# Attention and maxout in one kernel: the first half's masks as products on VectorE instead of sums on TensorE, in a new order of work

## The chip, the core and the metric

The kernel runs on one core of a Trainium2 chip. The metric is device time in microseconds; the time of a version is the median of several executions. One further execution was taken by the hardware profiler, and all rows of the profile are from that one. The engines are TensorE (PE, with its weight loads shown as PEld), VectorE (DVE), ScalarE (ACT), GpSimd (POOL) and SyncE (SP). In this kernel SP issues the transfers. They work on SBUF, and TensorE writes its results into eight PSUM banks. Each engine runs its own instructions in their written order and waits for the others at semaphores.

## What is computed

Four sequences of 768 tokens, 8 heads of 64 dimensions. Three heads are "retrieval" heads with a plain causal mask. The five others attend to a window of 64 tokens and to the first four tokens (the sinks). A maxout layer follows.

```python
scores = scale * np.matmul(q, k.transpose(0, 1, 3, 2))
causal = rel >= 0
stream_keep = causal & ((pos[None, :] < n_sink) | (rel < window))
mask = np.where(retr, causal, stream_keep)
scores = np.where(mask, scores, -1e9)
a = softmax(scores)                     # over the keys
x = (a @ v).transpose(0, 2, 1, 3).reshape(B * S, H * D)
g = np.maximum(x @ w1, x @ w2)
out = g @ w_out
```

## The kernel before

**Maxout.** max(x w1, x w2) is relu(x (w1 - w2)) + x w2. The kernel therefore prepares three weights: `w12` = w1 - w2 (four VectorE subtractions, L1184), `w2o` = w2 w_out, and `wob`, w_out in bf16. For `w2o` it casts w2 to bf16 (`w2b`), transposes it on TensorE (L1201), copies it to `w2t`, and multiplies it with `wob` (L1228, 32 matmuls in 16 steps: four banks times four quarters of `wob`). `wob` comes in quarters 0 to 3; each has its own transfer (`load_down`, L568) and its own cast, made by whichever engine the order names. A copy or cast that ScalarE does is recorded at L382, one by another engine at L384.

**Halves.** The work is done in eight halves of 384 queries, sequence by sequence or nearly: (0,0), (1,0), (0,1), (1,1), (2,0) and so on. For each half, q and k are cast to bf16, transposed (on TensorE at L680 in the first halves, by DMA later) and copied out of PSUM. Then come

- scores (`scores`, L959): key blocks by query blocks of 128, written into two banks at a time, in a number of groups t,
- exponentials (`exp`, L978, ScalarE) into the tile `at`, one per bank; no maximum is subtracted,
- masks (`mask`, L997, VectorE): `at` times a 0/1 table, in place,
- weighted sums (`weighted`, L1022, TensorE): `at` times v with a column of ones,
- the reciprocal (L1039) and the product with it (`normalise`, L1049, VectorE), which give `x`,
- the transposes of x (L1148, or by DMA), the up-projection with `w12` (`up`, L1251, eight blocks of four matmuls), the ReLU (L1276 on ScalarE or L1278 on VectorE), and the down-projection (`down`, L1308, 12 matmuls for each of three tiles of 128 rows), copied out and stored (L1336).

In the very first half the rows of v arrive in another layout; ScalarE, VectorE and GpSimd cast them into the tile `xt` (`cast_rows`, L720), and TensorE rearranges them (L723).

**Masks of the first half.** The first half (0,0) has groups of its own (`GROUP_A`). Streaming heads have blocks "near" (the diagonal and the window) and "far" (only sinks). Here no mask is multiplied: GpSimd writes tables of 0 and -1e30 into `tab` (`mask_table`, L1649 to L1662, over zeros that VectorE's memset at L1699 wrote), and TensorE puts them into the bank first, as a matmul of the identity and the table (L928). The scores then accumulate on it, and the exponential gives 0 where the table has -1e30. The other halves multiply, with 0/1 tables that GpSimd derives from the first ones by four comparisons (`kept`, L612).

**The order of work.** The order is one string, `PLAN`, written out by hand or by a search. A token such as `76p01` means operation 76 on TensorE with PSUM banks 0 and 1; a, v, g and s stand for ScalarE, VectorE, GpSimd and SP. `x0*40` means 40 dummy matmuls (L372) into bank 0: products of a zero tile, which nobody reads. `Order.run` emits the tokens one by one, so the string fixes the queue of every engine. The tables of costs and ranks beside it had a part in the search, not in what is emitted. SP's queue begins with q, k and v of the first half, and the weights follow: w2 in halves, w_out in quarters, w1 in halves. A transfer waits for the casts that free its place in the tile `ld`: w_out's quarters take the place of the first half's q, k and v.

Of the kernel before, what the change touches and what calls it, by code (L numbers as in the profile page):

```python
# [38 lines left out]
def one(p, hh, blocks):  # L39
# [16 lines left out]
B_FAR, B_NEAR, B_WIN, B_CAUSAL = 0, 2, 5, 7  # L56
GROUP_A = [
    (both(0, DIAG0 + f(0, 1)), [], [(0, 0, 1, B_CAUSAL, 3), (1, 0, 1, B_CAUSAL, 3)]),
    (
        [one(1, 0, DIAG0 + f(0, 1)), one(1, 1, NEAR)], [],  # L60
        [(0, 0, 1, B_CAUSAL, 3), (1, 0, 4, B_NEAR, 1)],
    ),
    (
        [one(0, 0, f(0, 2) + f(1, 2)) + one(1, 0, f(0, 2) + f(1, 2)),
         one(0, 1, f(0, 2) + f(1, 2)) + one(1, 1, FAR)], [], [(1, 2, 2, B_FAR, 1)],
    ),
    (both(2, NEAR), [], [(0, 0, 4, B_NEAR, 1), (1, 0, 4, B_NEAR, 1)]),
    (both(3, NEAR), [], [(0, 0, 4, B_NEAR, 1), (1, 0, 4, B_NEAR, 1)]),
    (
        [one(2, 0, FAR) + one(3, 0, FAR), one(2, 1, FAR) + one(3, 1, FAR)], [],  # L70
        [(0, 0, 2, B_FAR, 2), (1, 0, 2, B_FAR, 2)],
# [3 lines left out]
    (both(0, DIAG0 + f(0, 1)), [(0, 2, 0, 3, "causal")], []),  # L75
    (both(0, f(0, 2) + f(1, 2)), [], []),
    ([one(1, 0, DIAG0 + f(0, 1)), one(1, 1, WIN0)], [(0, 1, 0, 3, "causal"), (1, 1, 0, 4, 0)], []),
    ([one(1, 0, f(0, 2) + f(1, 2)), one(1, 1, d(2) + d(2))], [(1, 1, 0, 1, "band")], []),
    (both(2, WIN0), [(0, 2, 0, 4, 0)], []),
    (both(3, WIN0), [(0, 2, 0, 4, 0)], []),  # L80
    (
        [one(2, 0, d(2)) + one(3, 0, d(2)), one(2, 1, d(2)) + one(3, 1, d(2))],
        [(0, 2, 0, 2, "band")], [],
    ),
]
TWICE = [(0, 0, 2, B_WIN, 2), (1, 0, 2, B_WIN, 2)]
GROUP1 = [
    (
        both(0, DIAG1 + f(4, 5)), [(0, 2, 0, 3, "causal")],
        [(0, 0, 1, B_CAUSAL, 3), (1, 0, 1, B_CAUSAL, 3)],  # L90
    ),
    (both(0, f(0, 3, 4, 5) + f(3, 4)), [], []),
    (both(0, f(1, 3, 4, 5) + f(3, 5)), [], []),
    (both(0, f(2, 3, 4, 5)), [], []),
    (
        [one(1, 0, DIAG1 + f(4, 5)), one(1, 1, WIN1)], [(0, 1, 0, 3, "causal"), (1, 1, 0, 4, 2)],
        [(0, 0, 1, B_CAUSAL, 3), (1, 0, 2, B_WIN, 2)],
    ),
    ([one(1, 0, f(0, 3, 4, 5) + f(3, 4)), one(1, 0, f(1, 3, 4, 5) + f(3, 5))], [], []),
    (  # L100
        [one(1, 0, f(2, 3, 4, 5)), one(1, 1, END1 + d(5))], [(1, 1, 0, 2, 2)],
        [(1, 0, 2, B_WIN, 1)],
    ),
    (both(2, WIN1), [(0, 2, 0, 4, 2)], TWICE),
    (both(3, WIN1), [(0, 2, 0, 4, 2)], TWICE),
    (
        [one(2, 0, END1) + one(3, 0, END1), one(2, 1, END1) + one(3, 1, END1)],
        [(0, 2, 0, 4, 2)], TWICE,
    ),
# [63 lines left out]
0s x0*3 1s x0*5 2s x0*40 3s 30a 32v 68g x0*3 70a 54v x0 48p0 62a 27g x1 72p1 49v x2*4 29g 60a 73v x2 64p2 x3*2  # L173
65a x3*2 52g x3*5 8s 31a 55v x3 61g x3*2 56p3 33a 53v x4*3 4s 63a x4*2 69g x4 50p4 71a 57v x5 66p5 51a 58p6
28g x7 74p7 67a 59v x0*2 26g 76p01 75a 25g 79p23 9s 34a 37v 78a 36v 6s 35v 39a 82p45 77a 41g 85p67 84a 40a
88p10 83a 86a 13s 119v 91p54 38a 123v 89a 11s 46p6 87a 93a 42p1 47v 92a 44p7 80a 43v 16s 124p4 81a 127v 120p6
45a 131v 128p5 125a 104p2 121v 106p 94p1 90a 96p 107v 5v 95p3 10g 100p 132p7 109v 105p4 97v 101v 110p 108v
# [48 lines left out]
"""  # L226

LAST = """
1079v 1082p 1080s 1074a 1083p 1075s 1086p5 1084v 1087p 1088p 1085s 1089a 1090a
"""  # L230


# [1539 lines left out]
```

## Time and profile before

| | us |
|---|---|
| median of 3 runs | 177.53 (176.96 to 178.75) |
| the profiled execution | 178.13 |
| its span, first to last instruction | 175.6 |
| TensorE busy | 167.5, 95% |
| ScalarE busy | 123.8, 71% |
| VectorE busy | 117.6, 67% |
| GpSimd busy | 35.4, 20% |

Times in rows count from the start of the span. "Idle before" is the time that the engine stood still just before an instruction, with what ended it. A row with xN stands for N instructions: in the timeline, the first number is its start, the second the time from its first start to its last end. Matmuls overlap one another, so the time of one in a group is its own latency; what a further one costs is the growth of the group's time. The clock granted to TensorE was 1.00 in nearly every slice.

### The profile page before, as it was taken

Reading aid. Unit: us, or ns where it says so; the run is one execution under the profiler, and the core shown is the slowest. Engines: PE = TensorE matmul, PEld = TensorE weight load, DVE = VectorE, ACT = ScalarE, POOL = GpSimd, SP = SyncE. Lnnn points to the kernel's source line nnn. Section 1 sums busy time; section 2 is a strip of 40 time slices with the busy share of each in tenths; the row PEclk is TensorE's granted clock in tenths of the full one; section 3 lists DMA queues with packets and bytes.
Section 4 is the critical chain, followed back from the end, with each engine's and each line's share of the span. In section 5 each row is a group of like instructions: output and inputs, shape, how many; then the busy total and the mean of one; then the engine's idle time right before and its main releaser. Section 6 shows DMA issues by size and latency. Waiting matters only on the chain.

```text
span 175.6 us, 4870 instructions
## 1 busy us (share of the span) xinstructions
PE 167.5 (95%) x1755; PEld 102.1 (58%) x1775; DVE 117.6 (67%) x327; ACT 123.8 (71%) x278; POOL 35.4 (20%) x80
## 2 busy tenths in 40 slices
PE   7899898999999999999999999999999999999993
PEld 7755644654675575667556546664665457545542
DVE  5546997876999587778978525895895377820511
ACT  3499416899899997999589789965749479214310
POOL 6850213411304803043301004200021000000000
PEclk9999999999999999999999999999999999999999
DMA  5999999999899999997299699245997236053104
GB/s 127 333 373 385 387 381 330 196 317 301 192 197 333 253 257 212 238 227 177 65 188 232 162 258 219 59 123 134 241 248 183 50 88 243 2 151 119 65 6 179
DMA packets 77661, 36.14 MB, mean 206 GB/s; under 512 B 59202, under 2 KB 72514, under 8 KB 77634
## 3 DMA queue, kind: packets, MB, share of 16 engines
q1 hardware_dynamic: 77488, 35.73, 76.7%
q8 instruction: 15, 0.25, 0.7%
q14 instruction: 12, 0.10, 0.2%
q10 hardware_dynamic: 146, 0.07, 0.1%
HBM read 25.17 MB, written 6.29 MB: 179 GB/s over the span
## 4 chain that ended last, share of the span: by engine, by line
PE 68%; DMA 11%; ACT 6%; issue 5%; POOL 4%; SPq 3%; DVE 2%; DVEq 0%; ACTq 0%; POOLq 0%
PE ps L1308 30%; PE ps L1251 21%; PE ps L959 7%; PE ps L1022 7%; DMA ld<-in_moe_w_out_dram 6%; DMA ld<-in_v_dram 4%; ACT at L978 4%; PE ps L680 2%; SPq L455 2%; POOL wob L384 2%; PE ps L1228 1%; POOL tab L612 1%; ACT ot L382 1%; ACT vb L382 1%; DMA raw<-in_is_retrieval_dram 1%
## 5 line engine op out<-in xcount | busy, mean ns | idle before, releaser
L978 ACT ACTIVATE at<-ps 128x512 bf16<-128x512 f32 (+2 forms) x134 | 64.8, 578 | 4.6 <-PE ps L959 4.1
L1251 PE MATMUL ps<-xt,w 128*128 128x384 bf16 x256 | 45.2, 326 | 0.1
L1308 PE MATMUL ps<-wob,g 128*128 128x512 bf16 (+2 forms) x192 | 43.8, 371 | 0.7 <-issue 0.3
L997 DVE TENSOR_TENSOR at<-at,tab 128x1024 bf16<-128x1024 bf16 (+5 forms) x49 | 25.1, 524 | 12.3 <-ACT at L978 11.4
L1251 PEld LDWEIGHTS <-w 128*128 128x128 bf16 x256 | 24.0, 98 | 15.9 <-issue 0.6
L1308 PEld LDWEIGHTS <-g 128*128 128x128 bf16 x200 | 18.3, 98 | 19.6 <-issue 0.2
L1278 DVE TENSOR_SCALAR g<-ps 128x384 bf16<-128x384 f32 x34 | 18.5, 553 | 13.5 <-PE ps L1251 13.0
L382 ACT COPY ot<-ps 128x512 f32<-128x512 f32 (+1 forms) x16 | 9.0, 571 | 22.5 <-PE ps L1308 19.1
L1308 PE MATMUL ps<-w2o,xt 128*128 128x512 bf16 (+2 forms) x90 | 24.0, 370 | 0.5
L384 POOL CAST qb<-ld 128x384 bf16 (+1 forms) x31 | 13.6, 472 | 53.3 <-DMA ld<-in_k_dram 28.4
L1049 DVE TENSOR_TENSOR x<-ps,rez 128x192 f32 x64 | 22.7, 354 | 2.0 <-DVE rez L1039 0.5
L1022 PEld LDWEIGHTS <-at 128*128 128x128 bf16 x477 | 17.9, 97 | 4.7 <-DVE at L997 0.3
L1022 PE MATMUL ps<-vb,at 128*128 128x65 bf16 x387 | 19.3, 194 | 0.0
L1276 ACT ACTIVATE g<-ps 128x384 bf16<-128x384 f32 x30 | 14.5, 495 | 6.6 <-PE ps L1251 6.4
L959 PE MATMUL ps<-qk 64*128 64x128 bf16 (+1 forms) x330 | 19.1, 229 | 0.0
L959 PEld LDWEIGHTS <-qk 64*128 64x128 bf16 x330 | 12.1, 94 | 9.2 <-issue 7.0
L382 ACT CAST qb<-ld 128x384 bf16 (+1 forms) x32 | 12.8, 458 | 2.1 <-DMA ld<-in_q_dram 1.7
L1308 PEld LDWEIGHTS <-xt 128*128 128x128 bf16 x100 | 8.8, 98 | 8.1
L382 ACT COPY qk<-ps 128x384 bf16<-128x384 bf16 (+1 forms) x17 | 10.2, 631 | 2.3 <-PE ps L680 1.9
L384 DVE COPY ot<-ps 128x512 f32<-128x512 f32 (+1 forms) x9 | 6.0, 672 | 7.3 <-PE ps L1308 6.4
L680 PE MATMUL ps<-tab,qb 128*128 128x128 bf16 x120 | 10.0, 219 | 0.7 <-POOL qb L384 0.4
L384 POOL CAST vb<-ld 128x192 bf16 x15 | 6.1, 421 | 20.3 <-issue 10.2
(76 smaller groups left out, 162.7 us busy)
## 6 DMA issues: line engine op xcount, KB each, us to landing
ld<-in_v_dram SPq DMA_DIRECT2D x21, 256.0 KB, 5.4
ld<-in_moe_w_dram SPq DMA_DIRECT2D x4, 1024.0 KB, 12.2
out_dram<-ot SPq DMA_DIRECT2D x16, 256.0 KB, 3.6
ld<-in_q_dram SPq DMA_DIRECT2D x5, 768.0 KB, 8.1
ld<-in_k_dram SPq DMA_DIRECT2D x5, 768.0 KB, 6.9
ld<-in_q_dram SPq DMA_DIRECT2D x9, 256.0 KB, 4.5
ld<-in_k_dram SPq DMA_DIRECT2D x9, 256.0 KB, 4.4
ld<-in_moe_w_out_dram SPq DMA_DIRECT2D x4, 512.0 KB, 11.0
```

The source lines that it names most:

```text
L382: nc.scalar.copy(out=out, in_=in_)
L384: eng[e].tensor_copy(out=out, in_=in_)
L680: nc.tensor.transpose(to[:, i], qbs[:, T["qb", n, hf] % NQB, t, i].rearrange("p h d -> p (h d)"), ident)
L959: nc.tensor.matmul(to.rearrange("p (i c) -> p i c", c=128), lhsT=lhsT, rhs=q_of(n, i, m)[rows], start=bk not in under, stop=True, skip_gro ...
L978: nc.scalar.activation(out=at[:, bk, 0:w], in_=bank(("ps", b, hf, t), part=bk)[:, 0:w], func=ACT.Exp, scale=scale,)
L997: eng[e].tensor_tensor(out=at, in0=at, in1=tbl, op=ALU.mult)
L1022: nc.tensor.matmul(po[:, hh, i - NT * hf, :], lhsT=ats[:, T["at", b, hf, t] % NAT, bk, e * 128:(e + 1) * 128], rhs=rhs, start=first, stop= ...
L1049: nc.vector.tensor_tensor(out=xs[:, HALVES.index((b, hf)) % NX, :, bass.ds(heads[2 * p + hh], 1), :], in0=po[:, hh, :, 0:D].unsqueeze(2), ...
L1251: nc.tensor.matmul(bank(key)[:, 0:HALF], lhsT=w[:, kc, fc * 128:(fc + 1) * 128], rhs=xts[:, HALVES.index((b, hf)) % NXT, :, kc, :], start= ...
L1276: nc.scalar.activation(out=g, in_=ph, func=ACT.Relu)
L1278: nc.vector.tensor_scalar_max(out=g, in0=ph, scalar1=0.0)
L1308: nc.tensor.matmul(bank(key)[:, cols], lhsT=lhsT, rhs=(w2o if kind == "x" else wob)[:, c, cols], start=(e == 0), stop=(e == len(steps) - 1),)
```

## The change

1. The first half's masks are no longer added. The matmuls at L928 go, with the tables of -1e30, the lists of biases in the groups and `biases`. The groups of the first half name masks instead, and VectorE multiplies `at` by 0/1 tables behind the exponentials: seven new products, five of them of the new kinds "near" and "far".
2. GpSimd writes 0/1 tables at once, over ones in place of zeros, so `kept` goes. The last two copies of `mask_table` now write three blocks each. The memset of 576 words becomes one of 64 words (the identity's zeros) and one of 1280 bf16 ones.
3. `PLAN` is new from beginning to end. There are 133 dummies instead of 81. The other matmuls are the same ones, with the same sizes.

```diff
 GROUP_A = [
-    (both(0, DIAG0 + f(0, 1)), [], [(0, 0, 1, B_CAUSAL, 3), (1, 0, 1, B_CAUSAL, 3)]),
-    (
-        [one(1, 0, DIAG0 + f(0, 1)), one(1, 1, NEAR)], [],
-        [(0, 0, 1, B_CAUSAL, 3), (1, 0, 4, B_NEAR, 1)],
-    ),
+    (both(0, DIAG0 + f(0, 1)), [(0, 2, 0, 3, "causal")]),
+    ([one(1, 0, DIAG0 + f(0, 1)), one(1, 1, NEAR)], [(0, 1, 0, 3, "causal"), (1, 1, 0, 4, "near")]),
     (
         [one(0, 0, f(0, 2) + f(1, 2)) + one(1, 0, f(0, 2) + f(1, 2)),
-         one(0, 1, f(0, 2) + f(1, 2)) + one(1, 1, FAR)], [], [(1, 2, 2, B_FAR, 1)],
+         one(0, 1, f(0, 2) + f(1, 2)) + one(1, 1, FAR)], [(1, 1, 2, 2, "far")],
     ),
-    (both(2, NEAR), [], [(0, 0, 4, B_NEAR, 1), (1, 0, 4, B_NEAR, 1)]),
-    (both(3, NEAR), [], [(0, 0, 4, B_NEAR, 1), (1, 0, 4, B_NEAR, 1)]),
+    (both(2, NEAR), [(0, 2, 0, 4, "near")]),
+    (both(3, NEAR), [(0, 2, 0, 4, "near")]),
     (
-        [one(2, 0, FAR) + one(3, 0, FAR), one(2, 1, FAR) + one(3, 1, FAR)], [],
-        [(0, 0, 2, B_FAR, 2), (1, 0, 2, B_FAR, 2)],
+        [one(2, 0, FAR) + one(3, 0, FAR), one(2, 1, FAR) + one(3, 1, FAR)], [(0, 2, 0, 4, "far")],
     ),
 ]
...
 PLAN = """
-0s x0*3 1s x0*5 2s x0*40 3s 30a 32v 68g x0*3 70a 54v x0 48p0 62a 27g x1 72p1 49v x2*4 29g 60a 73v x2 64p2 x3*2
+0s x0*3 1s x0*5 2s x0*36 3s 66a 50v x0*3 28a 64v x0 48g x0 58a x0 68p0 26a 25g x1*2 52p1 56a 69v 44p2 x3 4s
...
-BIASED = ((0, 0),)
...
-    ident, bias, smask = tab[:, 0:128], tab[:, 128:1152], tab[:, 1152:1920]
-    causal = tab[:, 1920:2048]
+    ident, smask, causal = tab[:, 0:128], tab[:, 640:1408], tab[:, 512:640]
+    far, near = tab[:, 128:384], tab[:, 384:1408].rearrange("p (n two c) -> p n two c", two=2, c=128)[:, :, 0]
...
-    kept(pairs_[:, 0:1], 3)
-    kept(pairs_[:, 1:6:2], 6, times=3)
-    kept(pairs_[:, 2:6:2], 4, blocks=2)
-    kept(causal.unsqueeze(1), 7)
...
     def scores(b, hf, t):
-            for bk, e, m, col, times in biased:
-                src = bias[:, 128 * col:128 * col + 128 * m]
-                to = bank(("ps", b, hf, t), part=bk)[:, e * 128:(e + m * times) * 128]
...
-                nc.tensor.matmul(to, lhsT=ident, rhs=src, start=True, stop=False, skip_group_check=True)
...
-                        start=bk not in under, stop=True, skip_group_check=True,
+                        start=True, stop=True, skip_group_check=True,
...
     def mask(b, hf, t, part):
-            if isinstance(which, str):
+            if which == "near":
+                at = at.rearrange("p h (m c) -> p h m c", c=128)
+                tbl = near[:, 0:blocks].unsqueeze(1).to_broadcast([128, count, blocks, 128])
+            elif which == "far":
+                at = at.rearrange("p h (m c) -> p h m c", c=256)
+                tbl = far.unsqueeze(1).unsqueeze(1).to_broadcast([128, count, blocks // 2, 256])
+            elif isinstance(which, str):
...
+def mask_table(nc, table, n_sink, window):
+    blocks = table.rearrange("p (n c) -> p n c", c=128)
+    def put(which, base, by_key, by_query, fill=0.0):
+        to = blocks[:, which]
+        nc.gpsimd.affine_select(
+            out=to, in_=to, pattern=[[0, to.shape[1]], [by_query, 128]], compare_op=ALU.is_ge, fill=fill, base=base,
+            channel_multiplier=by_key,
+        )
+    sinks, both_, causal, diagonal = slice(0, 1), slice(1, 3), slice(3, 4), slice(4, 10, 2)
...
+    mixed = blocks[:, 5:10:2]
+    for rows, which in ((slice(0, 64), 0), (slice(64, 128), 1)):
+        nc.gpsimd.tensor_copy(out=mixed[rows], in_=blocks[rows, which:which + 1].to_broadcast([64, 3, 128]))
...
-    nc.vector.memset(tab[:, 0:1152], 0.0)
+    nc.vector.memset(tab[:, 0:128], 0.0)
+    nc.vector.memset(tab[:, 128:1408], 1.0)
```

**What moves, on TensorE** around the end of the weights' preparation. Names: `wob,w2t` is the product for `w2o` (line 1228 before, 1183 now), `tab,x` a transpose of the first half's x, `xt,w_144` (now `xt,w_139`) the up-projection, `warmer` a dummy, `vb,at` a weighted sum. Before:

```order
L1228 MATMUL ps_161<-wob,w2t 128x512
L1148 LDWEIGHTS x
L1148 MATMUL ps_164<-tab,x 128x128
...
L1148 MATMUL ps_167<-tab,x 128x128
L1228 LDWEIGHTS w2t
L1228 MATMUL ps_161<-wob,w2t 128x512
...
L1228 MATMUL ps_162<-wob,w2t 128x512
L1251 LDWEIGHTS w_144
L1251 MATMUL ps_165<-xt,w_144 128x384
```

And now:

```order
L980 MATMUL ps_160<-vb,at 128x65
L353 LDWEIGHTS warmer
...
L1183 MATMUL ps_161<-wob,w2t 128x512
...
L1183 MATMUL ps_159<-wob,w2t 128x512
L1206 LDWEIGHTS w_139
L1206 MATMUL ps_160<-xt,w_139 128x384
...
L1183 LDWEIGHTS w2t
L1183 MATMUL ps_158<-wob,w2t 128x512
```

Before, the eight products with the last quarter of `wob` stood directly behind the twelve transposes, and the up-projection behind them. Now 29 dummies stand behind the last weighted sum, then sixteen products with the transposes among them, then one block of the up-projection, and only then the eight products with the last quarter. The first cast of that kind that they wait for, quarter 1, was ScalarE's and is now GpSimd's; the last quarter's is GpSimd's in both.

**On ScalarE**, up to the last exponential of the first half (line 978 before, 930 now). Before:

```order
L978 ACTIVATE at<-ps_163 128x512
L382 CAST vb<-ps_167 128x8x64
L382 COPY w2t<-ps_164 128x1024
L978 ACTIVATE at<-ps_160 128x512
L382 CAST wob<-ld 128x1024
```

And now:

```order
L930 ACTIVATE at<-ps_159 128x512
L366 COPY w2t<-ps_162 128x1024
L930 ACTIVATE at<-ps_157 128x512
L366 CAST w2b<-ld 128x4x256
L930 ACTIVATE at<-ps_158 128x512
L366 COPY w2t<-ps_160 128x1024
L366 COPY w2t<-ps_157 128x1024
```

A cast of the second half of w2 now stands in front of the last exponential. Of the casts of v into `xt`, ScalarE keeps one of four. Over the whole program ScalarE takes 37 ReLUs instead of 30, and VectorE 27 instead of 34.

**On SP**, the loads of the weights (`in_moe_w` is w2 twice, then w1 twice). Before:

```order
L442 DMA ld<-in_v_dram 128x8x192
L547 DMA ld<-in_moe_w_dram 128x4x512 x2
L568 DMA ld<-in_moe_w_out_dram 128x2x512 x3
L547 DMA ld<-in_moe_w_dram 128x4x512
L568 DMA ld<-in_moe_w_out_dram 128x2x512
```

And now:

```order
L426 DMA ld<-in_v_dram 128x8x192
L531 DMA ld<-in_moe_w_dram 128x4x512
L552 DMA ld<-in_moe_w_out_dram 128x2x512
L531 DMA ld<-in_moe_w_dram 128x4x512
L552 DMA ld<-in_moe_w_out_dram 128x2x512 x2
```

The first of w_out's quarters now goes ahead of the second half of w2; behind these two the order is the old one.

More of the change, by code (lines that the diff above doesn't have):

```diff
@@ L74 @@
 GROUP0 = [
[L75 to L80, printed above, removed]
+    (both(0, DIAG0 + f(0, 1)), [(0, 2, 0, 3, "causal")]),
+    (both(0, f(0, 2) + f(1, 2)), []),
+    ([one(1, 0, DIAG0 + f(0, 1)), one(1, 1, WIN0)], [(0, 1, 0, 3, "causal"), (1, 1, 0, 4, 0)]),
@@ L312 @@
 SHARED = 0.89
-BIAS_TURNS = 0.21
 UP_PARTS = 2
@@ L369, in bank, with dummy @@
         return a if dtype == F32 else a.bitcast(dtype)
-    def dummy(e):
-        nc.tensor.matmul(banks[e][:, 0:128], lhsT=warm, rhs=warm, start=True, stop=True)
+    def dummy(e, m=1):
+        nc.tensor.matmul(
+            banks[e][:, 0:128 * m].rearrange("p (m c) -> p m c", m=m), lhsT=warm,
+            rhs=warm.unsqueeze(1).to_broadcast([128, m, 128]), start=True, stop=True,
+        )
     order = Order(dummy)
@@ L1093, in attend @@
             exps[t] = list(both_)
-            for part in group[t][1] if (b, hf) not in BIASED else ():
+            for part in group[t][1]:
                 cols = 128 * part[1] * part[3]
```

201 lines of the change are left out of this document (80 added, 121 removed).

## The prediction

> **What bounds the kernel now.** I read the busy table first, then the windows, then the chain of waits, and only then single rows.
>
> ```profile
> span 175.6 us, 4870 instructions
> PE 167.5 (95%) x1755; PEld 102.1 (58%) x1775; DVE 117.6 (67%) x327; ACT 123.8 (71%) x278; POOL 35.4 (20%) x80
> ```
>
> A share of 95% is an average over two different programs. The windows separate them; the columns are the stretch, its length, busy time of PE, PEld, DVE, ACT and POOL with counts, the granted PE clock, the DMA share and GB/s.
>
> ```profile
> 10.00:30.00 20.00, 18.08 (x196) 10.16 (x195) 14.80 (x31) 12.01 (x25) 4.54 (x5) 1.00 1.06 375
> 30.00:170.00 140.00, 138.64 (x1439) 82.62 (x1456) 96.31 (x269) 106.16 (x241) 23.13 (x52) 1.00 0.75 182
> 50.00:60.00 10.00, 9.95 (x85) 5.59 (x82) 8.62 (x23) 9.86 (x24) 5.26 (x12) 1.00 1.08 294
> 70.00:80.00 10.00, 10.00 (x144) 7.00 (x141) 7.73 (x19) 9.96 (x23) 2.76 (x6) 1.00 1.09 232
> ```
>
> From 30 to 170 TensorE is idle for 140.00 - 138.64 = 1.36 us in all: that stretch is matmul work, and its length hardly depends on anybody else. ScalarE is nearly full too in two of its stages (9.86 and 9.96 of 10). Up to 30 the transfers run flat out (a DMA share of 1.06, 375 GB/s), and TensorE fills gaps with dummy matmuls. The chain of waits says where the first program hands over to the second.
>
> ```profile
> 9.45 10.85 DMA ld<-in_moe_w_out_dram
> 20.35 1.04 POOL wob L384
> 21.39 4.33 issue
> 25.77 2.11 POOL wob L384
> 27.92 1.89 PE ps L1228 x8
> 29.81 3.25 PE ps L1251 x20
> 33.06 0.50 PE ps L680 x9
> ```
>
> Until 27.92 us the end is set by the landing of the output weight (the 4.33 us called issue is GpSimd waiting for its last quarter), then by GpSimd's cast of it. After that comes matmul on matmul. So the change is worth what it does to the time at which the dense part starts, and to the 1.36 us of idle time inside it. What it saves on TensorE before 27.92 is worth nothing in itself.
>
> **The change part by part: TensorE's tables.** It removes eleven L928 matmuls. The groups by form have ten of them (one record is missing); next to them, two rows of the timeline give the price of the dummies, whose number goes from 81 to 133.
>
> ```profile
> L928 PE MATMUL ps<-tab 128*128 128x512 bf16 x6 | 2.0, 383 | 0.2 <-ACT at L978 0.2
> L928 PE MATMUL ps<-tab 128*128 128x384 bf16 x3 | 0.8, 329 | 0.0
> L928 PE MATMUL ps<-tab 128*128 128x256 bf16 x1 | 0.3, 283 | 0.0
> 7.23 0.83 PE L372 MATMUL ps<-warmer 128*128 128x128 bf16 x12
> 9.12 0.22 PE L372 MATMUL ps<-warmer 128*128 128x128 bf16 x1
> ```
>
> Removed: 2.0 + 0.8 + 0.3 = 3.1 us. Added: a further dummy costs (0.83 - 0.22) / 11 = 0.055 us, and 52 of them 2.9 us. Both lie in the first 28 us, so this exchange is 0 on the path, as long as no dummy stands in front of work that is ready. Twenty-nine of them stand together, and I come back to these.
>
> **GpSimd and the memset.** GpSimd loses the four L612 table instructions, 0.85 + 2.16 = 3.0 us. VectorE's first memset grows from 576 elements (0.54 us) to 64 and 1280, by that row's rate 0.06 + 1.20 us. The tables then start some 0.7 us later, and GpSimd's first cast of q with them.
>
> ```profile
> 1.08 0.54 DVE L1699 MEMSET tab<- 128x576 uint32 x1 [1.08 <-PEq L1753]
> 6.33 0.85 POOL L612 TENSOR_SCALAR tab<-tab 128x256 bf16<-128x256 bf16 x1
> 8.92 2.16 POOL L612 TENSOR_SCALAR tab<-tab 128x128 bf16<-128x128 bf16 x3
> 8.28 1.11 ACT L382 CAST qb<-ld 128x192 bf16 x4 [0.37 <-DMA ld<-in_k_dram]
> ```
>
> The landing of k at 8.28 covers this: whatever is done with q before that waits for k. If GpSimd came later than 8.28, each microsecond would go on to the scores. I take 0, with ends 0 and 0.5.
>
> **VectorE's masks.** Seven products are added: three of 1024 columns and one each of 768, 512, 384 and 256. The rows of the later halves, which are masked in this way already, price them. The last two rows are ScalarE's casts of v and the last exponential of the first half.
>
> ```profile
> L997 DVE TENSOR_TENSOR at<-at,tab 128x1024 bf16<-128x1024 bf16 x18 | 12.1, 688 | 1.3 <-ACT at L978 1.0
> L997 DVE TENSOR_TENSOR at<-at,tab 128x768 bf16<-128x768 bf16 x7 | 3.9, 555 | 4.8 <-ACT at L978 4.6
> L997 DVE TENSOR_TENSOR at<-at,tab 128x512 bf16<-128x512 bf16 x10 | 4.7, 466 | 2.7 <-ACT at L978 2.2 <-POOL vb L384 0.3
> L997 DVE TENSOR_TENSOR at<-at,tab 128x384 bf16<-128x384 bf16 x7 | 2.6, 376 | 3.2 <-ACT at L978 3.1
> L997 DVE TENSOR_TENSOR at<-at,tab 128x256 bf16<-128x256 bf16 x4 | 1.4, 361 | 0.0
> L382 ACT CAST xt<-ld 128x192 bf16 x4 | 1.4, 350 | 0.1
> 18.35 0.71 ACT L978 ACTIVATE at<-ps 128x512 bf16<-128x512 f32 x1
> ```
>
> They add 3 x 0.688 + 0.555 + 0.466 + 0.376 + 0.361 = 3.8 us. VectorE has 20.00 - 14.80 = 5.2 us free between 10 and 30, so they fit. What counts is the last pair. Ahead of its last exponential ScalarE loses three casts of v and gains one of 1024 columns (three of 0.35 are 1.05; a cast of that size takes it 1.04, the second row of the next fence), so I leave that exponential's end at 18.35 + 0.71 = 19.06. The pair of 1024 column masks behind it, 1.4 us, ends at 20.5, and the weighted sums that wait for it (36 such matmuls took 1.27 us in the first row below; some twelve are left here) at 20.9.
>
> **The handover.** The rows that price it:
>
> ```profile
> 18.82 1.27 PE L1022 MATMUL ps<-vb,at 128*128 128x65 bf16 x36
> 21.68 1.04 ACT L382 CAST wob<-ld 128x1024 bf16<-128x1024 f32 x1 [2.62 <-DMA ld<-in_moe_w_out_dram]
> 25.74 2.13 POOL L384 CAST wob<-ld 128x1024 bf16<-128x1024 f32 x1 [4.34 <-DMA ld<-in_moe_w_out_dram]
> 25.76 1.22 DVE L1184 TENSOR_TENSOR w<-ld 128x1024 bf16<-128x1024 f32 x1
> 26.23 0.83 PE L1148 MATMUL ps<-tab,x 128*128 128x128 bf16 x12
> 27.92 1.89 PE L1228 MATMUL ps<-wob,w2t 128*128 128x512 bf16 x8 [0.86 <-POOL wob L384]
> 50.40 5.38 PE L1251 MATMUL ps<-xt,w 128*128 128x384 bf16 x32
> 31.05 0.64 POOL L384 CAST qb<-ld 128x192 bf16 x2 [3.18 <-DMA ld<-in_q_dram]
> ```
>
> Before, TensorE has 0.86 us of nothing to do ahead of 27.92. In the new order a block of the up-projection (four matmuls, 32 took 5.38, so 0.65 us with little to spare) stands ahead of the product that waits, and can fill it. Now the new queue from 20.9 on: 29 dummies (1.6 us) to 22.5. Then the products with the second quarter of the output weight: it landed at 21.68, and its cast moves from ScalarE (1.04) to GpSimd, which took 1.04 and 2.13 for such casts. So it is ready between 22.7 and 23.8; I take the middle, 23.3. Then sixteen products at (1.89 - 0.38) / 7 = 0.216, 3.45 us, to 26.75; twelve transposes, 0.65, to 27.4; the block, 0.65, to 28.05. The last quarter is ready at 27.87 as before. The eight products that waited end at 29.8, with one block already done. Before, the same work ended at 29.81 + 0.65 = 30.46. That is 0.7 us gained; 0.86 if GpSimd takes 1.04, and 0.15 if it takes 2.13. I take 0.5, the middle of these two ends.
>
> One thing follows at once: an earlier TensorE reaches the transposes of the next half earlier, which need its q, and q landed at 31.05. They stood at 33.06, four blocks (2.6 us) behind the handover in both orders, and casting takes about 1 us, so some 1 us of slack covers 0.5.
>
> [...]
>
> **The sum.** The profiled execution took 178.13 us, 2.5 around its span of 175.6; it is 0.6 above the median of 177.53. Tables and dummies 0, GpSimd and memset 0, masks 0, handover -0.5, dense part 0 (the same matmuls in another order; 1.36 us is all that there is to win): 178.13 - 0.5 = 177.6, which is 177.0 on the scale of the median.
>
> **The rivals.** *The new order also closes the dense part.* The handover gives its most and part of the 1.36 us goes too: -0.86 - 0.7 = 176.0, and at the very most -2.2 = 175.3. For it: TensorE alone bounds that stretch. Against it: little is left to win.
>
> *The handover comes late.* SP now issues the first quarter of the output weight (512 KB, 1.4 us at 375 GB/s) ahead of the second half of w2. ScalarE's new cast needs that half, and stands in front of the last exponential:
>
> ```profile
> 17.61 1.29 DVE L384 CAST w2b<-ld 128x1024 bf16<-128x1024 f32 x2 [0.76 <-DMA ld<-in_moe_w_dram]
> ```
>
> Landing at 17.61 + 1.4 = 19.0 puts the end of that cast at 20.0, of the exponential at 20.7, of the masks at 22.1, of the sums at 22.5, and of the dummies, which TensorE runs ahead of everything behind them, at 24.1. With the same steps from there (3.45 + 0.65 + 0.65 + 1.73) the work ends at 30.6, 0.1 later than before. It decides from a start at 24.0 on; with a further mask late (0.7) it gives 177.5 + 0.8 = 178.3, slower than before. For it: the dummies stand in the queue whether TensorE has time or not. Against it: the row does not show whether w2's half was alone in flight or shared the DMA engines with that quarter, in which case it lands where it did.
>
> *ScalarE becomes the bound.* In the whole program it takes seven more of the ReLU rows and gives up two of its copies of 768 columns:
>
> ```profile
> L1276 ACT ACTIVATE g<-ps 128x384 bf16<-128x384 f32 x30 | 14.5, 495 | 6.6 <-PE ps L1251 6.4
> L382 ACT COPY qk<-ps 128x768 bf16<-128x768 bf16 x8 | 6.3, 797 | 1.4 <-PE ps L680 1.1 <-DVE kx L384 0.3
> ```
>
> That is 7 x 0.495 = 3.5 us more and 2 x 0.797 = 1.6 us less. If all of the 1.9 us falls where ScalarE is full, TensorE waits for banks: 177.53 + 1.9 = 179.4. It decides where ScalarE's share passes 10 of 10. For it: 9.86 and 9.96. Against it: most of the ReLUs may stand elsewhere.
>
> That the change does not do what it says is no rival with a time of its own: the dummies that stand in for the removed matmuls are already in the sum.
>
> **How the numbers follow.** My forecast has 0.5, the closed dense part 0.17, the late handover 0.18, ScalarE 0.15. The bound for the three outcomes is 1%, 1.8 us, about what a measurement of this kernel can tell from no change. Faster by that needs under 175.8, most of all that can be won: 0.13. Slower needs over 179.3, ScalarE's case or a stall in the new order that I can't see: 0.14. That leaves 0.73 within 1%. The range runs from 175.6, the closed dense part nearly in full, to 179.1, most of ScalarE's case.
>
> **What would show it.** Right: no L928 group; the first products with the second quarter between 22.7 and 24; one block of the up-projection ahead of the wait for GpSimd's last cast, and that wait gone; the end of those eight products plus one block 0.1 to 0.9 us ahead of 30.46; 138 to 139 us of PE in the 140 us from 30 on. Wrong: more than 2.5 us idle in that stretch, ScalarE above 9.9 in it with TensorE waiting for it, or that same work ending later than 30.5.

## The result, and the profile after

| | before | now |
|---|---|---|
| median of the comparison, 9 executions each | 177.76 us (176.96 to 178.75) | 176.41 us (176.11 to 177.18) |
| ratio, with its 95% interval | | 0.9934 (0.9910 to 0.9958) |
| the profiled execution; its span | 178.13; 175.6 | 177.18; 175.4 |
| all executions with a span on record (111 and 16): median time | 177.59 | 176.42 |
| median span (lowest to highest) | 175.1 (174.3 to 177.0) | 174.65 (174.3 to 175.4) |
| time outside the span (lowest to highest) | 2.45 (2.38 to 2.60) | 1.73 (1.67 to 1.84) |

Left out here and below as slow are one execution of the kernel before (218.22 us, at a granted clock of 0.76), one of experiment 7 (182.05, at 0.95) and one of experiment 9 (194.91, at 0.855).

The kernel is 0.7% faster, 1.2 us. That is within 1% of no change, and 0.6 us below the forecast. The last two rows are the surprise: of the 1.17 us between the two large medians, 0.45 lie inside the span and 0.72 outside it, between the profile's first and last instruction and the ends of the measured time. The outside part is nearly the same in every single execution of a kernel, and my sum had no term for it.

The busy table of the new kernel, and its window over the dense part, whose columns are those of the prediction's windows:

```profile
span 175.4 us, 4945 instructions
PE 168.5 (96%) x1795; PEld 105.5 (60%) x1816; DVE 122.0 (70%) x331; ACT 126.3 (72%) x280; POOL 34.2 (19%) x78
```

```profile
30.00:170.00 140.00, 138.67 (x1437) 82.77 (x1454) 96.94 (x268) 107.09 (x243) 22.57 (x50) 1.00 0.77 181
50.00:60.00 10.00, 9.92 (x94) 6.07 (x92) 9.71 (x26) 9.72 (x25) 5.13 (x11) 1.00 1.00 270
80.00:90.00 10.00, 9.89 (x141) 5.99 (x139) 7.01 (x26) 9.93 (x25) 1.16 (x2) 1.00 0.55 131
```

TensorE's 138.67 us answer to 138.64 before: by this view nothing happened there. Two further profiles show what the view is worth. The first line is the kernel before and the second the new one, both unchanged:

```profile
30.00:170.00 140.00, 139.79 (x1455) 82.52 (x1454) 95.25 (x269) 105.40 (x239) 23.15 (x52) 1.00 0.75 181
```

```profile
30.00:170.00 140.00, 139.82 (x1458) 82.86 (x1456) 96.47 (x268) 107.18 (x243) 22.80 (x50) 1.00 0.77 181
```

The same kernel shows 1439 matmuls in one profile and 1455 in another, and its weight loads, 1456 and 1454, show that it executed about the same number. Most of the 1.36 us that I called idle were matmul records missing from the trace.

The handover in the new kernel, first SP's queue, then rows of the timeline in order of time:

```profile
7.31 0.37 SPq L552 DMA_DIRECT2D ld<-in_moe_w_out_dram  x1
7.72 0.47 SPq L531 DMA_DIRECT2D ld<-in_moe_w_dram  x1
...
18.72 1.04 ACT L366 CAST w2b<-ld 128x1024 bf16<-128x1024 f32 x1 [0.83 <-DMA ld<-in_moe_w_dram]
...
19.68 0.59 ACT L930 ACTIVATE at<-ps 128x512 bf16<-128x512 f32 x1
19.99 1.60 DVE L955 TENSOR_TENSOR at<-at,tab 128x384 bf16<-128x384 bf16 x3
...
21.45 1.04 POOL L368 CAST wob<-ld 128x1024 bf16<-128x1024 f32 x1 [4.37 <-DMA ld<-in_moe_w_out_dram]
21.62 1.43 DVE L368 CAST wob<-ld 128x1024 bf16<-128x1024 f32 x1
21.65 0.54 PE L980 MATMUL ps<-vb,at 128*128 128x65 bf16 x12 [0.15 <-DVE at L955]
...
22.13 1.78 PE L353 MATMUL ps<-warmer 128*128 128x128 bf16 x29
...
23.75 1.89 PE L1183 MATMUL ps<-wob,w2t 128*128 128x512 bf16 x7
...
25.29 5.46 DVE L1139 TENSOR_TENSOR w<-ld 128x1024 bf16<-128x1024 f32 x4
25.42 0.49 PEld L1103 LDWEIGHTS <-x 128*128 128x128 bf16 x8 [0.28 <-DVE x L1007]
25.46 1.94 POOL L368 CAST wob<-ld 128x1024 bf16<-128x1024 f32 x1 [2.96 <-DMA ld<-in_moe_w_out_dram]
...
27.87 0.81 PE L1206 MATMUL ps<-xt,w 128*128 128x384 bf16 x4
...
28.52 1.89 PE L1183 MATMUL ps<-wob,w2t 128*128 128x512 bf16 x8
```

This is the late handover of my rivals, nearly number by number: the half of w2 at 18.72 (there 19.0), the end of the last exponential at 20.27 (20.7), the masks at 21.59 (22.1), the sums at 22.2 (22.5), the dummies at 23.9 (24.1), the end of the eight products at 28.52 + 1.89 = 30.41 (30.6). One block of the up-projection stands ahead of them, at 27.87, and TensorE no longer waits for GpSimd's last cast. Before, the same work ended at 30.46.

### The profile page after: what moved, and what is told of

It reads as the page before. It is cut to its first block, busy times and chain, and to the rows that moved or that the text cites. A ratio compares the mean times of both kernels' runs of the same rounds, so it can differ in the third digit from the quotient of the medians.

```text
span 175.4 us, 4945 instructions
## 1 busy us (share of the span) xinstructions
PE 168.5 (96%) x1795; PEld 105.5 (60%) x1816; DVE 122.0 (70%) x331; ACT 126.3 (72%) x280; POOL 34.2 (19%) x78
## 4 chain that ended last, share of the span: by engine, by line
PE 85%; DMA 6%; POOL 3%; issue 2%; DVE 2%; POOLq 0%; ACT 0%; DVEq 0%; SPq 0%; ACTq 0%
PE ps L1263 36%; PE ps L1206 24%; PE ps L915 9%; PE ps L980 8%; DMA ld<-in_moe_w_dram 6%; PE ps L645 3%; PE ps L1183 3%; POOL tab L1605 1%; PE ps L1103 1%; DVE at L955 1%; PE ps L353 1%; DVE x L1007 0%; POOL tab L1619 0%; POOL g L705 0%; POOLq L1670 0%
## 5 line engine op out<-in xcount | busy, mean ns | idle before, releaser
L1263 PE MATMUL ps<-wob,g 128*128 128x512 bf16 (+2 forms) x192 | 44.7, 370 | 0.4
L955 DVE TENSOR_TENSOR at<-at,tab 128x1024 bf16<-128x1024 bf16 (+5 forms) x56 | 29.9, 549 | 10.7 <-ACT at L930 10.3
L1206 PEld LDWEIGHTS <-w 128*128 128x128 bf16 x256 | 23.9, 98 | 16.0 <-issue 0.4
L1231 ACT ACTIVATE g<-ps 128x384 bf16<-128x384 f32 x37 | 18.0, 502 | 11.1 <-PE ps L1206 10.0
L1233 DVE TENSOR_SCALAR g<-ps 128x384 bf16<-128x384 f32 x27 | 14.6, 550 | 15.8 <-PE ps L1206 15.7
L368 POOL CAST qb<-ld 128x384 bf16 (+1 forms) x28 | 13.2, 505 | 50.5 <-DMA ld<-in_q_dram 30.6
L366 ACT COPY ot<-ps 128x512 f32<-128x512 f32 (+1 forms) x18 | 10.4, 575 | 17.0 <-PE ps L1263 16.8
L980 PE MATMUL ps<-vb,at 128*128 128x65 bf16 x387 | 20.4, 193 | 0.4 <-DVE at L955 0.4
L368 DVE COPY qk<-ps 128x384 bf16<-128x384 bf16 (+1 forms) x17 | 11.3, 693 | 3.9 <-PE ps L645 3.8
L366 ACT CAST qb<-ld 128x384 bf16 (+1 forms) x31 | 11.8, 440 | 2.8 <-DMA ld<-in_q_dram 1.7
L353 PE MATMUL ps<-warmer 128*128 128x128 bf16 x133 | 12.1, 256 | 1.4 <-POOL warmer L1655 1.2
L353 PEld LDWEIGHTS <-warmer 128*128 128x128 bf16 x133 | 10.5, 118 | 1.7 <-POOL warmer L1655 1.2
```

Source lines behind the costliest of these rows:

```text
L353: nc.tensor.matmul(banks[e][:, 0:128 * m].rearrange("p (m c) -> p m c", m=m), lhsT=warm, rhs=warm.unsqueeze(1).to_broadcast([128, m, 128]) ...
L366: nc.scalar.copy(out=out, in_=in_)
L368: eng[e].tensor_copy(out=out, in_=in_)
L955: eng[e].tensor_tensor(out=at, in0=at, in1=tbl, op=ALU.mult)
L980: nc.tensor.matmul(po[:, hh, i - NT * hf, :], lhsT=ats[:, T["at", b, hf, t] % NAT, bk, e * 128:(e + 1) * 128], rhs=rhs, start=first, stop= ...
L1206: nc.tensor.matmul(bank(key)[:, 0:HALF], lhsT=w[:, kc, fc * 128:(fc + 1) * 128], rhs=xts[:, HALVES.index((b, hf)) % NXT, :, kc, :], start= ...
```

## Experiments

Below, "the handover" is the time at which the eight products with the last quarter of the output weight and one block of the up-projection are done (a block takes 0.65), and "the rest" is the span minus that.

**1. The kernel before, once more (before_again).** Nothing is edited.

> The kernel before, unchanged, to see its span over several executions. The kernel now had spans of 174.4 to 175.4 us with some 1.75 us outside them; the one execution of the kernel before that has a span shown had 175.6, and 2.5 outside. Theory A (the gain lies in the work itself, and the profiled execution of the new kernel was one of its slow ones): spans of 175.7 to 176.3 with 1.7 to 1.8 outside. Theory B (most of the gain lies outside the span, in starting and ending the program): spans of 175.0 to 175.6, with 2.3 to 2.5 outside in all executions.

Measured: 177.50 us (176.75 to 178.91, 12 executions), spans of 174.3 to 176.4 with a median of 175.1, and 2.38 to 2.60 outside. Theory B holds for the time outside. But the spans vary by 2 us, and this profile, whose span is 174.3, shows why. The rows are from the timeline:

```profile
25.30 1.04 POOL L384 CAST wob<-ld 128x1024 bf16<-128x1024 f32 x1 [4.35 <-DMA ld<-in_moe_w_out_dram]
25.34 2.07 DVE L1184 TENSOR_TENSOR w<-ld 128x1024 bf16<-128x1024 f32 x1
...
26.46 1.89 PE L1228 MATMUL ps<-wob,w2t 128*128 128x512 bf16 x8
```

GpSimd's cast of the last quarter took 1.04 and VectorE's subtraction 2.07, where the prediction's profile had 2.13 and 1.22. The handover is at 26.46 + 1.89 + 0.65 = 29.00, in place of 30.46. The other 0.4 us were there before that cast began: it started at 25.74 then and at 25.30 here, and the second of VectorE's two casts of the second half of w2 started at 18.22 and 17.80. So my base for the handover was one execution among differing ones, and a late one.

**2. Without the 29 dummies (no_dummies).**

```diff
-105v x2*4 7g x2*2
-106v x2*7 110v x2*2 114v x2*2 112v x2*6 111v x2*6 14s 140p
+105v 7g
+106v 110v 114v 112v 111v 14s 140p
```

> The new kernel without the 29 dummies behind the last weighted sums. My prediction put them on the path (1.6 us). Theory A (dummies on the path): the first products with the second quarter of the output weight start at 22.5, when its cast is ready, in place of 23.8, and the eight products with the last quarter end at 29.1 in place of 30.4; the time falls by 1.0 to 1.3. Theory B (x sets the end there: the transposes of x waited 0.28 us for VectorE's normalisation, which ends at 25.36): eight products run earlier, then TensorE stands still until 25.4, and the time changes by less than 0.2. A wait of 1.0 us or more for VectorE ahead of the transposes would show B.

Measured: 176.44 us (175.96 to 176.83), as with them (176.41). TensorE's rows:

```profile
22.48 2.00 PE L1183 MATMUL ps<-wob,w2t 128*128 128x512 bf16 x8 [0.37 <-POOL wob L368]
...
25.35 0.62 PE L1103 MATMUL ps<-tab,x 128*128 128x128 bf16 x8 [0.88 <-DVE x L1007]
...
28.41 1.89 PE L1183 MATMUL ps<-wob,w2t 128*128 128x512 bf16 x8
```

The products start 1.3 us earlier, and then TensorE waits 0.88 for x. Theory B holds: the dummies fill a gap that VectorE sets, and the handover stays at 30.30.

**3. The second half of w2 ahead of the first quarter again (w2_first).**

```diff
- ... 44p2 x3 4s
+ ... 44p2 x3
-60p3 53v x4*2 45v x4*5 8s 29a
+60p3 53v x4*2 45v x4*5 8s 4s 29a
```

> The new kernel with SP's transfer of the second half of w2 put back ahead of the first quarter of the output weight. Both theories expect the second half at about 17.6 in place of 18.7, and the last exponential of the first half about 1 us earlier. Theory A (the late handover of my prediction costs what I gave for it): the work behind it moves too, and the time falls by 0.7 to 1.0. Theory B (dummies, and the cast of a quarter of the output weight that VectorE makes ahead of the normalisation at 21.6, hold the path anyway): VectorE waits for that quarter to land, x is ready within 0.3 of 25.4, and the time changes by less than 0.3.

Measured: 178.62 us (178.21 to 180.34), 2.2 slower, which neither theory had. The half does land early, and the exponential runs 1.07 us earlier:

```profile
18.61 0.64 ACT L930 ACTIVATE at<-ps 128x512 bf16<-128x512 f32 x1
18.66 1.04 POOL L368 CAST wob<-ld 128x1024 bf16<-128x1024 f32 x1 [6.57 <-DMA ld<-in_moe_w_out_dram]
18.74 2.38 DVE L955 TENSOR_TENSOR at<-at,tab 128x384 bf16<-128x384 bf16 x3
...
19.75 1.46 PE L1183 MATMUL ps<-wob,w2t 128*128 128x512 bf16 x6 [2.39 <-POOL wob L368]
```

In the new kernel GpSimd's cast of the first quarter of the output weight stood earlier:

```profile
16.04 1.04 POOL L368 CAST wob<-ld 128x1024 bf16<-128x1024 f32 x1 [3.82 <-DMA ld<-in_moe_w_out_dram]
```

That quarter is now cast at 18.66, and TensorE's queue has its products in front of the weighted sums: it stands still for 2.39 us. SP's order and TensorE's order are one decision; what I counted as the cost of SP's order buys that cast. The three masks took 2.38 us beside GpSimd's cast, where they had taken 1.60.

**4. x earlier: the cast of the third quarter on ScalarE, and no dummies (wob2_scalar).** On top of experiment 2:

```diff
-138p3 132a 113p 104v 10v 107p5
+138p3 132a 10a 113p 104v 107p5
```

> The new kernel without the 29 dummies, and with the cast of the third quarter of the output weight moved from VectorE (1.43 us ahead of the normalisation) to ScalarE, which stands idle for 4 us there. If x is what sets the handover, it is ready at about 23.9 in place of 25.4, TensorE has no wait ahead of its transposes, and the eight products with the last quarter end near 29.2 in place of 30.4: the time falls by 0.7 to 1.2, the lower end because q of the next half is cast only by 32.1 to 32.7. If the landing of the last quarter (25.5) and of that q set the pace of everything behind, the time falls by less than 0.3, and the gain shows up again as a wait of TensorE for q before 33.

Measured: 176.27 us (175.40 to 177.37), median span 174.6, the same as the new kernel. The profile is of its fastest execution, with a span of 173.7:

```profile
24.30 0.61 PE L1103 MATMUL ps<-tab,x 128*128 128x128 bf16 x8
...
27.35 1.89 PE L1183 MATMUL ps<-wob,w2t 128*128 128x512 bf16 x8
...
32.13 0.34 PEld L645 LDWEIGHTS <-qb 128*128 128x128 bf16 x6 [0.30 <-ACT qb L366]
```

x was what held the transposes: they stand at 24.30 without a wait, and the handover is at 29.24, 1.1 earlier. Then TensorE reaches the transposes of the next half before their q is cast (0.30 us). The spans now spread from 173.7 to 175.7, where the new kernel's spread from 174.3 to 175.4. The time fell by less than 0.3, the second outcome of the expectation. That the gain of 1.1 is lost to this wait in the typical execution is likely; one profile doesn't show it.

**5. The tables' matmuls alone (before_no_sums).** The kernel before:

```diff
     def biases(b, hf, t):
-        return group_of(b, hf)[t][2] if (b, hf) in BIASED else ()
+        return ()
```

> The kernel before without its eleven matmuls that add the tables (L928), nothing in their place, so the first half is left unmasked. Theory A (my prediction: up to the handover TensorE's own work is worth nothing): the time stays within 0.3 of the kernel before, and the 2.45 us outside the span stay. Theory B (the sums stood on the path): 0.5 us or more faster, with the exponentials of the first half ending earlier.

Measured: 177.65 us, ratio 1.0004 (0.9984 to 1.0024), spans as before (median 175.15), 2.43 outside. With nothing in their place, the first half is left unmasked; the later work is the same. Theory A holds: TensorE's eleven matmuls cost nothing that the interval (0.3 us less to 0.4 us more) can tell.

**6. The mechanism without the new order (before_masks).** The kernel before with the new tables, `kept` emptied, no L928, and the products placed behind the exponentials:

```diff
     def exp(b, hf, t, bk):
         def emit(_):
...
+            if (b, hf) == (0, 0):
+                ready.add((t, bk))
+                for part in MASKED_A[t][1]:
+                    banks_ = {(t, i) for i in range(part[0], part[0] + part[1])}
+                    if (t, bk) in banks_ and banks_ <= ready:
+                        mask(b, hf, t, part)("DVE")
```

> The whole mechanism of the change in the old order: new 0/1 tables, no L928, no GpSimd comparisons, the two memsets, and the seven products on VectorE, each placed right behind the last exponential that it needs. Theory A (the mechanism is worth nothing by itself, my prediction, and the gain comes from the new order): spans as those of the kernel before, median 175.0, within 0.3. Theory B (masks on VectorE cost something where they stand, and the new order hides it): 0.5 to 1.5 slower spans, by masks behind the last exponential that delay the weighted sums and x. The time outside the span tells whether its 0.7 us belong to the mechanism (1.75 here) or to the order (2.45 here).

Measured: 178.50 us (177.90 to 179.11), ratio 1.0057 (1.0033 to 1.0080); median span 176.4, so 1.3 longer; 2.09 outside. Theory B holds. ScalarE, VectorE and TensorE at the handover:

```profile
19.51 0.62 ACT L988 ACTIVATE at<-ps 128x512 bf16<-128x512 f32 x1
...
20.16 1.37 DVE L1019 TENSOR_TENSOR at<-at,tab 128x1024 bf16<-128x1024 bf16 x1
...
21.59 0.54 PE L1044 MATMUL ps<-vb,at 128*128 128x65 bf16 x12 [0.34 <-DVE at L1019]
...
28.50 1.89 PE L1250 MATMUL ps<-wob,w2t 128*128 128x512 bf16 x8
```

The last weighted sums start at 21.59 (20.37 in the prediction's profile of before), 1.2 later, behind 1.4 us of masks. Part of that is not the masks': in this profile the page gives a granted clock of 0.6 for the slice from 13.2 to 17.6 us. It gives the same in experiment 5's, which has no masks there; its last sums start at 20.64, so 0.95 of the delay is left. The spans don't rest on that stretch: the four executions at a clock of 1.00 have 176.2 to 177.1. The masks are not free in the old order; the new one has to earn that back. The handover is at 31.04.

**7. Six more entries into the scores (split_scores).** The new kernel, one dummy in the middle of each of six runs of score matmuls:

```diff
-372p01 ... 388p31 ... 493p21 ... 502p75 ... 518p73 ... 634p61
+x0 372p01 ... x3 388p31 ... x2 493p21 ... x7 502p75 ... x7 518p73 ... x6 634p61
```

> The new kernel with six single dummies, each put into the middle of a run of score matmuls behind 46 us. From 30 us on the old order enters the scores (matmuls of 64 rows among matmuls of 128) 24 times, the new one 22 times, and each entry shows a weight load that waited 0.3 to 0.4 us for nothing the trace names. Theory A (an entry costs TensorE that time, and two entries fewer are 0.7 to 0.8 us of the gain): six more entries cost 6 x 0.39 + 6 x 0.055 = 2.7 us. Theory B (the wait is covered by matmuls still running): six dummies cost 0.3 us and no more.

Measured: 178.03 us (177.61 to 178.39, 11 executions); spans of 175.9 to 176.7, median 176.3, so 1.65 more than the new kernel. Less the dummies' 0.33, an entry and the return from it cost 0.22 us: neither 0.39 nor nothing. This takes a dummy by itself to cost the 0.055 us that a further one costs in a row of dummies. A single dummy among matmuls of 128 rows was not tried, so what belongs to the change of size and what to a dummy standing alone is not separated. TensorE's weight loads and what they waited for, from 30.3 on, in the kernel before, the new one and this one:

```profile
PEld L959 <- issue: 5.4, 14, 0.4
...
PEld L680 <- POOL qb L384: 0.5, 1, 0.5
```

```profile
PEld L915 <- issue: 4.7, 12, 0.4
```

```profile
PEld L915 <- issue: 5.1, 13, 0.4
...
PEld L353 <- issue: 0.3, 2, 0.2
```

The columns are the sum, the number and the longest wait. Not each entry shows such a wait, as I had written, but 14 of 24 in the kernel before. In the new order the row has 12 waits in both profiles of the new kernel and 14 in experiment 9's, which enters the scores once less, so the view names the place and not the price. The 0.22 us for an entry and the return from it is my estimate, on the condition above; what TensorE does in that time no run here shows.

**8. The new kernel, once more (after_again).** Nothing is edited.

> The new kernel unchanged, for a profile at full clock (the first had 0.997 and a span of 175.4, where six others at full clock had 174.4 to 174.7). Both theories expect a median of 176.4. If the clock alone made the difference, the work behind the weights' preparation ends at the same 30.3 to 30.4 us and the rest is shorter by 0.7; if the transfers differ from execution to execution, it ends earlier, near 29.8.

Measured: 176.42 us (176.00 to 176.84, 7 executions); the profile has a span of 175.0 at a clock of 1.00, and the handover at 30.44. In the five profiles with this handover, with the dummies or without, it lies between 30.25 and 30.44. Neither theory holds. The handover is the same and the rest is 144.6 in place of 145.0, but the clock is not why: in the first profile it was lower in the last microsecond alone (0.50 from 174.5 on, where TensorE has no work), and experiment 2's profile, at 0.997 too, has a rest of 144.6. Load by load, the first profile falls behind this one by 0.14 us at 45.7 and by a further 0.22 at 66.4, each time at weighted sums that wait for VectorE's masks. Rows of the second place, first of the first profile, then of this one:

```profile
65.33 1.04 DVE L955 TENSOR_TENSOR at<-at,tab 128x1024 bf16<-128x1024 bf16 x1
...
66.42 0.29 PEld L980 LDWEIGHTS <-at 128*128 128x128 bf16 x8 [0.16 <-DVE at L955]
```

```profile
65.19 0.82 DVE L955 TENSOR_TENSOR at<-at,tab 128x1024 bf16<-128x1024 bf16 x1
```

In the first profile GpSimd's casts of q began at 65.32, 0.01 ahead of its mask at 65.33: this looks like the meeting of VectorE and GpSimd of experiment 1 again.

**9. Moved and merged (best).** On top of experiment 4, a part of the down-projection is moved behind the scores that it split:

```diff
-252p72 234p 254a ... 264p27 258a
+252p72 254a ... 264p27 234p 258a
```

> The new kernel without the 29 dummies, with the cast of the third quarter of the output weight on ScalarE, and with one entry into the scores less (a part of the down-projection moved behind the run that it split). Theory A (an entry costs 0.25 us, as the six added ones did, and an earlier handover is worth what the trace showed in its best execution): median span 174.6 - 0.25 = 174.35 at most, down to 173.4; time 175.1 to 176.1. Theory B (what is gained at the handover is given back to waits for transfers, and one entry can't be seen): 176.2 to 176.5.

Measured: 176.16 us (175.70 to 177.56, 11 executions), ratio 0.9931 (0.9905 to 0.9956); median span 174.5. That lies between the ranges of the two theories and can't be told from the new kernel. The profile has the handover at 29.30, and TensorE's weight loads wait for q:

```profile
PEld L645 <- POOL qb L368: 1.1, 2, 0.6
...
PEld L645 <- ACT qb L366: 0.4, 1, 0.4
```

Of 1.1 us won at the handover, 1.5 us of such waits can take all; this is one profile, of an execution with a span of 174.9. They start behind 31.73, where the new kernel reaches its first transposes of q at 32.85.

**10. The place of the program's end, new kernel (moved_end).** Instructions that never run, in the branch that isn't taken:

```diff
     with known.Else():
         tile_any_heads(tc, *anyhow, room=room)
+        for _ in range(3):
+            nc.gpsimd.memset(room["g"][:, 0:8], 0.0)
+        for _ in range(6):
+            nc.scalar.activation(out=room["h1"][:, 0:8], in_=room["h1"][:, 0:8], func=ACT.Copy)
...
```

> The new kernel with instructions added to its fallback branch only, which stands between the main program and the program's end and is not executed here: 3 on GpSimd, 6 on ScalarE, one transfer of SP, 251 on VectorE and 174 on TensorE. [...] Theory A (the 0.7 us outside the span come from where the code of the program's end lies): 2.4 us outside the span. Theory B (they come from what is executed): 1.75 as in the new kernel, and its span too, 174.4 to 174.7.

Measured: 177.27 us (176.71 to 177.41); median span 174.8, about as in the new kernel, and 2.40 to 2.56 outside in all eight executions. Theory A, to the hundredth: 2.44 as in the kernel before. With nothing else executed, 0.7 us of the gain are gone.

**11. The same on the kernel before (before_moved_end).** The same kind of edit, with 249 instructions on GpSimd, 250 on ScalarE, 5 on VectorE and 82 on TensorE.

> [...] Theory A (the place of the end's code makes the time outside the span): 1.75 outside, spans as before (median 175.2), time 176.9, 0.7 less with the same work. Theory B (what made the difference in the experiment on the new kernel was something else in the added instructions, their number, say): 2.4 or more outside.

Measured: 176.86 us (175.98 to 178.38), ratio 0.9964 (0.9931 to 0.9996); median span 175.15 as before, and 1.68 to 1.78 outside. Theory A again: the kernel before becomes 0.7 us faster by instructions that it does not execute. Its profile is of its slowest execution (span 176.7), with 1.3 us of stalls in the program's last matmuls that no other profile has, so its rest (146.7) is left out below. It also has the other outcome of the meeting in experiment 1, from the timeline:

```profile
25.33 1.22 DVE L1184 TENSOR_TENSOR w<-ld 128x1024 bf16<-128x1024 f32 x1
25.36 2.09 POOL L384 CAST wob<-ld 128x1024 bf16<-128x1024 f32 x1 [4.40 <-DMA ld<-in_moe_w_out_dram]
...
27.50 1.89 PE L1228 MATMUL ps<-wob,w2t 128*128 128x512 bf16 x8 [0.87 <-POOL wob L384]
```

**12. 128 instructions on four engines (best_moved).** Experiment 9 with 128 never executed instructions for each of four engines.

> [...] The span should stay (median 174.5). [...]

Measured: 176.13 us (175.61 to 176.94), ratio 0.9930 (0.9908 to 0.9952); median span 174.35, 1.69 to 1.84 outside. There is no further step to win by this shift. It is the lowest median of the study, but 0.3 us below the new kernel's is within what these runs can't tell. Experiment 9 executes the same work; the 21 spans of the two have a median of 174.4, against 174.65, which would fit an entry of 0.25 and does not show it.

## Why the prediction was right, and where it was not

Its outcome, within 1%, and the range came true. That its -0.5 agrees with the -0.45 measured inside the span is luck: it stood for an earlier handover, which did not come, and the gain lies in two places that the sum held at no change, the dense part and the time outside the span.

- **Tables and dummies, 0.** Right: a ratio of 1.0004 without the tables' matmuls (experiment 5). That the dummies stand on the path, as my queue had them, was wrong: x stands behind them (experiment 2).
- **GpSimd and the memset, 0.** Right. The second memset took 1.12 where I had worked out 1.20, GpSimd's tables started 0.6 later, and the casts of k still began at 8.28:

```profile
1.31 1.12 DVE L1657 MEMSET tab<- 128x1280 bf16 x1 [0.21 <-issue]
...
8.31 0.64 POOL L368 CAST qb<-ld 128x192 bf16 x2 [0.72 <-DMA ld<-in_k_dram]
```

- **Masks, 0 on the path.** The seven products took 4.3 us where I had 3.8 (three of 0.691, and 0.816, 0.741, 0.348 and 0.292). VectorE's masks of all halves went from 25.1 to 29.9 us, so those of the later halves took longer too. The step "I leave that exponential's end at 18.35 + 0.71 = 19.06" failed. ScalarE's new cast of w2 stands ahead of it and waited for a transfer that had been moved back, so the exponential ended at 20.27; with the transfer put back (experiment 3) it ended at 19.25. I had this as a rival, worked out right to 0.5 us, and gave it 0.18, because I thought that the half might have shared the DMA engines with the quarter. In the old order the mechanism costs 1.3 us of span (experiment 6).
- **GpSimd's cast of the second quarter.** It took 1.04, the better of my two values. VectorE's masks were done by 21.59, 0.14 after it started, so they hardly ran beside it. Beside it ran VectorE's cast of a quarter, which started 0.17 later and took 1.43, where such a cast, with GpSimd's cast not yet begun, took 0.65 in the kernel before (at 19.58).
- **Handover, -0.5.** Wrong as a term. The new order's handover is at 30.25 to 30.44; the old order's was at 29.00, 29.59, 30.04 and 30.46 in four profiles. So the new one is as late as the latest of the old: against the 30.46 that I started from it gains 0.05, short of the 0.1 to 0.9 that I had named as the sign, and against the middle of the four it loses some 0.6. The median spans, less the middle of the rests below, put the typical ones nearer together, at 175.1 - 145.2 = 29.9 and 174.65 - 144.6 = 30.05. The step that failed is the exponential's end, above, and with it the base: one execution.
- **Dense part, 0.** Wrong. The rest took 145.1 to 145.3 in four profiles of the old order (the kernel before twice, experiments 5 and 6). In the new order it took 144.5 to 145.0, but for experiment 7 and for experiment 9 with its waits for q. Some 0.6 us come from there, by the middle of these profiles; experiment 8 shows that 0.4 can come and go between two executions of one kernel. Two entries into the scores fewer (22 for 24 from 30 us on) would be worth 0.44 at 0.22 each. The old order's wait for q at L680 does not explain the difference: it is 0.5 in the prediction's profile, but the profiles of experiments 5 and 6 have none and the same rest. What makes up the 0.6 was not tried by itself and stays open. I had ruled this out with "1.36 us is all that there is to win", from the busy time of matmuls. It counts a matmul's own latency as busy (0.38 us for one of 512 columns, where a further one of a group costs 0.22) and missing records as idle, so it bounds nothing.
- **ScalarE, no bound.** Right: it reaches 9.93 of 10 between 80 and 90, with TensorE at 9.89, and 9.94 in the profile of experiment 8, with TensorE at 10.00.
- **What lies around the span.** I wrote "2.5 around its span" and carried it over. It became 1.73, and 0.72 is more than all the rest of the gain.

In sum I forecast -0.5 in the wrong place. What happened inside the span is -0.45: by these profiles some -0.6 in the dense part, and a loss of about 0.15 at the typical handover. Outside it is -0.72. The mechanism of the change is a loss in the old order, the new order pays for it, and more than half of what is measured is where the program's end came to lie.

## What to carry to other kernels

Split a difference of less than 1% into span and time outside before looking for its cause, and take the second from several executions: this program, with a branch ahead of its end, gained and lost 0.7 us by code that it never runs (experiments 11 and 10). Before a row becomes a term of a sum, look whether it is a meeting of two engines that 0.04 us can turn round; if it is, its two outcomes are the bounds. And when two queues are re-ordered together, price the pair: the late transfer that looked like the cost of the new order was what kept TensorE fed.

## What the runs showed of the hardware

- **The end's code.** The time outside the span took the values 2.44 (2.38 to 2.60), 2.09 (2.01 to 2.20) and 1.73 (1.66 to 1.84). It moves between 1.71 and 2.44 when never executed instructions shift the end, both ways (experiments 10 and 11). The numbers of instructions that they add follow an assumption of mine on which shifts count, which the two results fit; neither that assumption nor what takes the time is shown by a run here. Two shifts of TensorE's code alone, by 22 matmul and weight-load instructions (experiment 5, 2.43) and by 58 (experiment 2, 1.73), changed nothing, and neither did 128 on each of four engines (experiment 12, 1.69 to 1.84). Half of the step probably belongs to VectorE or GpSimd: the profile with 2.09 outside (experiment 6) counts TensorE's instructions of experiment 5 and ScalarE's of the kernel before, and only VectorE's and GpSimd's differ (335 and 76, for 327 and 80). The engines were not moved one by one.
- **Two engines meeting.** When GpSimd's cast started 0.04 us ahead of VectorE's subtraction, it took 1.04 and the subtraction 2.07 (experiment 1); when it started 0.03 behind, it took 2.09 and the subtraction 1.22 (experiment 11). Apart, they took 1.04 and 1.23 (the kernel before, at 20.35 and 24.35). In these rows the first to start kept that time, and the other ended as if it had waited for the first's end: GpSimd, when second, ended 0.89 to 0.90 behind VectorE's end (the prediction's profile and experiment 11), and VectorE 1.07 behind GpSimd's (experiment 1). It does not hold as a rule: in experiment 5 the cast started 0.58 ahead and still took 1.30, with VectorE's product for x beside it from 25.64 on, and the subtraction took 1.79 and ended 1.07 behind the cast's end. At 0.02 us the recorded starts don't tell who is first: GpSimd's cast is recorded 0.02 ahead in the prediction's profile and in experiment 3's, and took 2.13 in the one and 1.04 in the other. The kernel before had this 0.04 us in front of its handover, which fits its spread of 174.3 to 177.0. In both profiles of the new kernel VectorE is ahead (25.29 against 25.46, and 25.31 against 25.48), and its spans spread over 1.1 us.
